# Two PSUM banks as one two-bank tile, or as two one-bank tiles taken in turn, in a fused retention and gated MLP kernel

## The chip, the cores and the metric

The kernel runs on one core of a Trainium2 chip, as one program. The metric is device time in microseconds (us) of one execution. Each engine of the core (TensorE, called PE in the profile; VectorE, DVE; ScalarE, ACT; GpSimd, POOL; SyncE, SP, which issues most transfers) works through its own queue in program order, and waits between engines go over semaphores.

## What is computed

```python
def _attn_ref(q, k, v):                       # 4 batches, 8 heads, 768 tokens, head size 64
    ...
    for t in range(S):
        state = gamma[None, :, None, None] * state + np.einsum('bhd,bhe->bhde', k[:, :, t], v[:, :, t])
        y[:, :, t] = scale * np.einsum('bhd,bhde->bhe', q[:, :, t], state)

def _moe_ref(x, w_val, conv_w, w_out):        # x: the y of all heads side by side, 512 wide
    ...
    for k in range(K):                        # K = 5 taps
        gate_pre += conv_w[k][None, None, :] * xp[:, k:k + S, :]
    gate = 1.0 / (1.0 + np.exp(-gate_pre))
    val = x @ w_val
    return (gate * val @ w_out).astype(np.float32)
```

## The kernel before

The 768 tokens of each batch are cut into 6 chunks of 128, which makes 24 blocks g of one batch and one chunk. The first four blocks (chunk 0) run as `wide_attention`, the others as `attention`: scores (L222) into the PSUM tile `sy`, a mask on DVE (`u`, L232), the state in `z_ps` (L244), a copy of it on ACT (`snap`, L254), and the block's y as the sum of `y_state` and `y_scores` (both L367). DVE multiplies y by a decay and writes it to `x` (`evac`, L435). When a chunk's four blocks are there, the chunk goes through the MLP: `x` is split into a rounded part `xh` (ACT, L444) and a rest `xl` (POOL, L448), DVE sums the taps of the convolution (L550), ACT takes the sigmoid (`gate`, L557).

**Products.** `val` (L565) makes one value tile of 128x512 out of 12 matmuls; DVE multiplies it by the gate (`gated`, L574, the rows `gate<-mm,gate`). The result is split again, into `gvh` (ACT, L581) and `gvl` (POOL, L585), and `outp` (L594) makes one output tile out of 12 matmuls, which ACT copies to `o_sb` (`store`, L604) and SP sends to memory. There are 24 value tiles and 25 output tiles (the last one is made in two halves).

**Banks.** All these sums lie in two PSUM banks, the tile `mm`, 128 x 2 x 512. A helper hands out its halves in turn:

```python
    mm = ps_m.tile([P, 2, 512], F32, name="mm")
    ...
    def bank_of(what):
        banks.append(what)
        return mm[:, (len(banks) - 1) % 2]
```

A value tile and an output tile are mostly summed side by side: PE's queue has matmuls of the one and of the other in alternation. The opening uses the same two banks for `outer`, `turn` and `wide_y`, read by DVE (L302) and ACT (L356, L359). The y of the seven blocks in `PAIRED` (10, 12, ... 22) is summed in both halves of `mm` at once, the y of other blocks in `sy`. The other tiles of PSUM are `sy` (2 banks), `z_ps` (2) and `acc` (2), so that all 8 banks are taken.

**Order.** Every engine's order is fixed by a table of step numbers, `TURNS`, which `plan` turns into the emission order under a manual schedule. Semaphore waits are not written by hand: the layer below places them, from which tiles an instruction reads and writes and which earlier instructions of other engines touched them. Loads of later blocks are held behind products by `hold` (four products back), and all loads and stores go through SP's one queue.

Of the kernel before, what the change touches and what calls it, by code (L numbers as in the profile page):

```python
# [7 lines left out]
F32 = mybir.dt.float32  # L8
# [5 lines left out]
ALU = mybir.AluOpType  # L14
PSUM = bass.MemoryType.PSUM

P = 128
HALF = 64
# [69 lines left out]
def tile_retention_gated_mlp(  # L88
# [32 lines left out]
    nc = tc.nc  # L121
    B, S, DM = out.shape
    NCH = S // P
    HALO = TAPS - 1
# [10 lines left out]
    ps_y = ctx.enter_context(tc.tile_pool(name="ps_y", bufs=1, space=PSUM))  # L135
    ps_s = ctx.enter_context(tc.tile_pool(name="ps_s", bufs=1, space=PSUM))
    ps_a = ctx.enter_context(tc.tile_pool(name="ps_a", bufs=2, space=PSUM))
    ps_m = ctx.enter_context(tc.tile_pool(name="ps_m", bufs=1, space=PSUM))

    tiny = const.tile([P, 1], F32, name="tiny")  # L140
    first_sb = const.tile([P, 512 + NPAIR * TAPS + 36, 2], I32, name="first_sb")
# [12 lines left out]

    z_ps = ps_s.tile([P, 2, B, 2, HALF], F32, name="z_ps")
    sy = ps_y.tile([P, 2, 512], F32, name="sy")
    mm = ps_m.tile([P, 2, 512], F32, name="mm")

    warm = nc.const_aps.tensor(0.0, (P, 1), F32).bitcast(BF16)[:, 0:1]
    steps = []  # L160
# [8 lines left out]
    ys = {}  # L169
    tiles, us, snaps, xs, xh, xl, decs, pos_ps = {}, {}, {}, {}, {}, {}, {0: base}, []  # L170
    rises, falls, begun, falling, turned = {}, {}, [], [], {}

    products = []
    banks, last_of = [], {}

    def bank_of(what):
        banks.append(what)
        return mm[:, (len(banks) - 1) % 2]

    def hold(dma):  # L180

# [23 lines left out]
    def halves(g, what):  # L205

        return tiles[g][:, what].rearrange("p x j (s t) -> p x j s t", s=2)
# [49 lines left out]
    def place(head):  # L257
        return next(
            (x, r, j) for x in range(2) for r in range(2) for j in range(2) if BY_DIM[x][r][j] == head
        )  # L260
# [28 lines left out]
        )  # L289

    def outer(r):
        ps = rises[r] = bank_of(r)
        for i in range(4):
            cols = slice((4 * r + i) * P, (4 * r + i + 1) * P)
            nc.tensor.matmul(
                ps[:, i * P:(i + 1) * P], lhsT=falling[0][:, 0, cols], rhs=falling[0][:, 1, cols],
                start=True, stop=True, skip_group_check=True,
            )
# [19 lines left out]
    def by_token(g, what):  # L318
        return tiles[g][:, what].rearrange("p x j (s e) -> p (x j s) e", s=2)

    def wide_y(g):
        if g not in ys:
            ys[g] = bank_of(g).rearrange("p (a t) -> p a t", t=P)
        v = by_token(g, 2)
        u = us.pop((g, 0)), us.pop((g, 1))
        for ct in range(NPAIR):
            for i, cols in enumerate((LO, HI)):
                x, r, j = place(2 * ct + i)
                nc.tensor.matmul(  # L329
                    ys[g][cols, ct], lhsT=v[:, 2 * ct + i], rhs=u[r][:, 2 * x + j],  # L330
                    start=True, stop=True, skip_group_check=True,
                )
# [13 lines left out]
    turned = {}  # L346

    def turn(g):
        turned[g] = bank_of(g).rearrange("p (a t) -> p a t", t=P)
        kT = tiles[g][:, 1]  # L350
        for x in range(2):
            for j in range(2):
                nc.tensor.transpose(turned[g][:, 2 * x + j], kT[:, x, j], eye_sb)
# [5 lines left out]
        nc.scalar.copy(xs[0][:, :, g, HALO:], ys.pop(g))  # L359

    def area_of(g):
        return ("mm", mm, 0) if g in PAIRED else ("sy", sy, 256)

    def y_mm(g, h, cols, j, s, lhsT, rhs, start):
        _, area, off = area_of(g)
        off += (2 * j + s) * HALF
        return nc.tensor.matmul(  # L367
            area[cols, h, off:off + HALF], lhsT=lhsT, rhs=rhs,
            start=start, stop=True, skip_group_check=True,
        )  # L370

    def behind(area, way):

        was, last = last_of.get(area, (way, None))
        if was != way:
            tc.add_manual_dep(
                nc.tensor.nop().ins, last.ins.name,
                mybir.DependencyInfo(mybir.DependencyClass.Sync, mybir.DependencyReason.DATA),
                reason="row tiles that share a bank",
            )  # L380

    def y_state(g, begins=True):
        if area_of(g)[0] == "mm":
            bank_of(g), bank_of(g)
        q = halves(g, 0)
        behind(area_of(g)[0], 0)
        for s in (1, 0):
            sn = snaps.pop((g, s))
            for j in range(2):
                for h, x, rows, cols in ((0, 0, LO, LO), (1, 0, HI, LO), (1, 1, LO, HI), (0, 1, HI, HI)):  # L390
                    last = y_mm(g, h, cols, j, s, sn[rows, x, j, :], q[rows, x, j, s, :], begins and s == 1 and j == 0)
        last_of[area_of(g)[0]] = 0, last

    def y_scores(g, begins=False):
        v, u = halves(g, 2), us.pop(g)
        behind(area_of(g)[0], 1)
        for s in range(2):
            for j in range(2):
                for h, x, rows, cols in ((0, 0, LO, LO), (1, 0, HI, LO), (1, 1, HI, HI), (0, 1, LO, HI)):
                    last = y_mm(g, h, cols, j, s, v[rows, x, j, s, :], u[rows, x, 2 * j + s, :], begins and s == 0 and j == 0)  # L400
        last_of[area_of(g)[0]] = 1, last

    def first_pos():
        pos_ps.append(ps_a.tile([P, 512], F32, name="acc"))
# [26 lines left out]

    def evac(g):
        b, c = chunks[g]
        _, area, off = area_of(g)
        nc.vector.tensor_tensor(  # L435
            xs[c][:, :, b, HALO:].rearrange("p (h j) t -> p h j t", h=2),
            area[:, :, off:off + 256].rearrange("p h (j t) -> p h j t", t=P),
            decs[c].rearrange("p (h j) t -> p h j t", h=2),
            op=ALU.mult,
        )  # L440

    def round_x(n, ct):
        xh[n, ct] = mlp.tile([P, B, P], F32R, name="xh", bufs=XS)
# [96 lines left out]
    accs, gate, gvs, vps, ops, outs = {}, {}, {}, {}, {}, {}  # L540
# [17 lines left out]

    def val(n, m, i):
        if i == 0:  # L560
            vps[n, m] = bank_of((n, m))
        ct = i % NPAIR
        w, xx = ((wvh, xh), (wvl, xh), (wvh, xl))[i // NPAIR]
        last_of.clear()
        products.append(nc.tensor.matmul(  # L565
            vps[n, m],
            lhsT=w[:, m, ct * P:(ct + 1) * P],
            rhs=xx[n, ct].rearrange("p b t -> p (b t)"),
            start=(i == 0), stop=(i == 3 * NPAIR - 1),
        ))  # L570
# [15 lines left out]

    def outp(n, b, i, cs):
        if i == 0:
            ops[n, b, cs.start] = bank_of((n, b))
        ct = i // 3  # L590
        gvh, gvl = gvs[n, ct]
        gg, w = ((gvh, woh), (gvh, wol), (gvl, woh))[i % 3]
        last_of.clear()
        products.append(nc.tensor.matmul(  # L594
            ops[n, b, cs.start][:, 0:cs.stop - cs.start],
            lhsT=gg[:, b * P:(b + 1) * P],
            rhs=w[:, ct, cs],
            start=(i == 0), stop=(i == 3 * NPAIR - 1),
        ))
# [82 lines left out]
    PAIRED = range(10, NG, 2)  # L682
# [25 lines left out]
    def wide_attention(g):  # L708

        before_block(g)  # L710
        qk, v, k = keys_of(g)
        sc, u, y, bank = Slot("s", 1), [Slot("gvl", GV), Slot("gvl", GV)], Slot("mm", 2), Slot("mm", 2)
        at("PE", 0.5, [qk, "eye"], [bank], turn, g)
        steps[-1].uses.append(held[g])
        at("ACT", 0.5, [bank], [k], take, g)
        steps[-1].uses.append(held[g])
        at("POOL", 1.0, ["small"], [k], decay, g)
        steps[-1].uses.append(held[g])
        at("PE", 1.0, [qk], [sc], wide_scores, g)
        steps[-1].uses.append(held[g])  # L720
        for r in range(2):
            at("DVE", 0.6, [sc, ("fall", r)], [u[r]], wide_mask, g, r)
            steps[-1].uses.append(table_of[r])
        at("PE", 1.0, [v] + u, [y], wide_y, g)
        steps[-1].uses.append(held[g])
        at("PE", 0.6, [v, k] + ["z0"] * (g > 0), [("z", g)] + ["z0"] * (g == 0), wide_state, g)
        steps[-1].uses.append(held[g])
        if g == 0:
            xbufs[0] = Slot("x", XB)
            at("POOL", 0.14, [], [xbufs[0]] + [("x", 0, i) for i in range(B)], new_x, 0)  # L730
        at("ACT", 0.5, [y, xbufs[0]], [("x", 0, g)], wide_evac, g)
        dec_of.setdefault(1, Slot("dec", 2))
        at("ACT", 0.3, ["base", "small"], [dec_of[1], ("dec", 1, g)], table, 1, g)
# [5 lines left out]
    def block(g):  # L739

        y_scores(g, True)
        state(g, 1)
        state(g + 1, 0)
        y_state(g, False)
        scores(g + 1)
# [133 lines left out]
    for r in range(2):  # L879
        bank = Slot("mm", 2)  # L880
        at("PE", 0.26, ["falling"], [bank], outer, r)
        steps[-1].uses.append(falling_of)
        at("DVE", 0.6, [bank, "wide"], [table_of[r], ("fall", r)], weigh, r)
# [124 lines left out]
```

## Time and profile before

| | us |
|---|---|
| median of 3 runs | 251.64 |
| lowest and highest run | 248.99, 251.9 |
| the profiled execution, its own time | 249.62 |
| its span, from the first instruction to the last | 247.9 |
| PE busy | 208.6 |
| DVE busy | 124.1 |
| ACT busy | 116.5 |
| POOL busy | 106.4 |

The durations of the next sections all come from the one profiled execution. Its time is 1.7 us more than its span and 0.8% under the median of the three runs. An engine counts as busy while it executes; waiting in its queue counts as idle, and the profile names the instruction that ended each idle stretch.

### The profile page before, as it was taken

How to read it: one execution, taken by the hardware profiler on the slowest of the kernel's cores; microseconds unless marked ns; L12 is line 12 of the kernel's file. 1: busy time of each engine (PE TensorE's matmuls, PEld its weight loads, DVE VectorE, ACT ScalarE, POOL GpSimd, SP SyncE). 2: the span in 40 equal slices, each digit the busy share in tenths (PEclk: the TensorE clock that was granted, in tenths of full speed). 3: DMA queues.
4: the chain of work that ended last, by engine and by line, in shares of the span. 5: the costliest groups of instructions: out<-in, count | busy, mean ns of one | idle time of the engine just before them, and what ended most of it. 6: DMA issues, size and time to landing. Idle time of an engine off the chain costs nothing.

```text
span 247.9 us, 7469 instructions
## 1 busy us (share of the span) xinstructions
PE 208.6 (84%) x3315; PEld 161.4 (65%) x3315; DVE 124.1 (50%) x188; ACT 116.5 (47%) x241; POOL 106.4 (43%) x99
## 2 busy tenths in 40 slices
PE   4976899996899889888989977898978778778773
PEld 2765688884577768666677865686856556556553
DVE  0755689996665616561636941555835424511000
ACT  4778979796536254344452336343232433302111
POOL 1358988899550538024291500960222540403000
PEclk9999799999799999999999999999999999999999
DMA  6997875587104733760002598010200201111032
GB/s 221 398 405 282 320 256 178 167 317 305 70 24 177 275 127 95 290 215 0 1 3 79 159 384 311 10 45 4 87 0 0 87 0 42 43 42 42 15 115 85
DMA packets 8402, 35.18 MB, mean 142 GB/s; under 512 B 937, under 2 KB 1193, under 8 KB 5810
## 3 DMA queue, kind: packets, MB, share of 16 engines
q1 hardware_dynamic: 8352, 34.66, 38.3%
q8 instruction: 26, 0.43, 0.7%
q10 hardware_dynamic: 18, 0.04, 0.1%
q14 instruction: 6, 0.05, 0.1%
HBM read 28.41 MB, written 6.29 MB: 140 GB/s over the span
## 4 chain that ended last, share of the span: by engine, by line
PE 74%; ACT 11%; DVE 7%; DMA 4%; issue 3%; ACTq 0%; SPq 0%; DVEq 0%
PE mm L594 28%; PE mm L565 28%; ACT o_sb L604 5%; DVE gate L574 5%; PE sy L367 4%; PE mm L367 4%; DMA out_dram<-o_sb 3%; PE sy L222 2%; PE z_ps L244 2%; PE sy L267 1%; PE mm L329 1%; DMA wst<-in_fall_dram 1%; ACT x L359 1%; DVE x L435 1%; ACT acc L488 1%
## 5 line engine op out<-in xcount | busy, mean ns | idle before, releaser
L550 DVE SCALAR_TENSOR_TENSOR acc<-x,cw_sb,acc 128x512 f32<-128x512 f32 x96 | 69.6, 750 | 7.1 <-ACT acc L548 6.2
L585 POOL TENSOR_TENSOR gvl<-gate,gvh 128x512 fp32r<-128x512 f32 x24 | 30.7, 1285 | 67.4 <-ACT gvh L581 57.9
L574 DVE TENSOR_TENSOR gate<-mm,gate 128x512 f32<-128x512 f32 x24 | 16.5, 690 | 63.4 <-PE mm L594 32.9
L594 PE MATMUL mm<-wol,gvh 128*128 128x512 f32 (+1 forms) x100 | 39.7, 405 | 9.5 <-DVE gate L574 5.4
L594 PE MATMUL mm<-woh,gvh 128*128 128x512 f32 (+1 forms) x100 | 39.5, 403 | 3.5 <-DVE gate L574 3.1
L604 ACT COPY o_sb<-mm 128x512 f32<-128x512 f32 (+1 forms) x25 | 13.9, 569 | 60.6 <-PE mm L565 27.5
L448 POOL TENSOR_TENSOR xl<-x,xh 128x512 fp32r<-128x512 f32 x24 | 30.5, 1287 | 26.6 <-ACT xh L444 26.5
L594 PE MATMUL mm<-woh,gvl 128*128 128x512 f32 (+1 forms) x100 | 39.1, 395 | 1.7 <-DVE gate L574 1.7
L565 PE MATMUL mm<-xh,wvh 128*128 128x512 f32 x96 | 31.2, 422 | 4.8 <-ACT o_sb L604 2.7
L212 POOL TENSOR_TENSOR att<-att,first_sb 128x512 f32<-128x512 f32 x24 | 24.9, 1043 | 20.8 <-ACT att L356 8.1
L565 PE MATMUL mm<-xl,wvh 128*128 128x512 f32 x96 | 30.7, 399 | 2.2 <-ACT o_sb L604 1.3
L565 PE MATMUL mm<-xh,wvl 128*128 128x512 f32 x96 | 31.1, 398 | 1.4 <-ACT o_sb L604 1.4
L594 PEld LDWEIGHTS mm<-wol,gvh 128*128 128x128 f32 x100 | 19.0, 190 | 17.1 <-DVE gate L574 7.4
L565 PEld LDWEIGHTS mm<-xh,wvh 128*128 128x128 f32 x96 | 18.0, 194 | 11.1 <-ACT o_sb L604 4.4
L594 PEld LDWEIGHTS mm<-woh,gvh 128*128 128x128 f32 x100 | 19.0, 192 | 9.0 <-DVE gate L574 4.5
L581 ACT CAST gvh<-gate 128x512 fp32r<-128x512 f32 x24 | 14.9, 621 | 20.4 <-DVE gate L574 12.0
L594 PEld LDWEIGHTS mm<-woh,gvl 128*128 128x128 f32 x100 | 19.0, 190 | 6.4 <-DVE gate L574 2.6
L565 PEld LDWEIGHTS mm<-xl,wvh 128*128 128x128 f32 x96 | 17.9, 188 | 7.7 <-ACT o_sb L604 2.2
L557 ACT ACTIVATE gate<-acc 128x512 f32<-128x512 f32 x24 | 14.3, 599 | 17.3 <-DVE acc L550 15.2
L565 PEld LDWEIGHTS mm<-xh,wvl 128*128 128x128 f32 x96 | 17.9, 188 | 6.1 <-ACT o_sb L604 2.2
L254 ACT COPY snap<-z_ps 128x256 f32<-128x256 f32 x40 | 14.1, 373 | 12.3 <-PE z_ps L244 10.9
L548 ACT ACTIVATE acc<-x,cw_sb 128x512 f32<-128x512 f32 x24 | 16.6, 696 | 5.1 <-DVE x L435 3.1
(64 smaller groups left out, 257.5 us busy)
## 6 DMA issues: line engine op xcount, KB each, us to landing
att<-in_att_dram SPq DMA_DIRECT2D x20, 1024.0 KB, 5.5
out_dram<-o_sb SPq DMA_DIRECT2D x23, 256.0 KB, 4.3
wst<-in_w_dram SPq DMA_DIRECT2D x7, 512.0 KB, 6.4
att<-in_att_dram SPq DMA_DIRECT2D x3, 768.0 KB, 8.3
first_sb<-in_first_dram SPq DMA_DIRECT2D x1, 568.0 KB, 6.3
att<-in_att_dram SPq DMA_DIRECT2D x1, 512.0 KB, 4.7
att<-in_att_dram SPq DMA_DIRECT2D x1, 256.0 KB, 7.4
out_dram<-o_sb SPq DMA_DIRECT2D x2, 128.0 KB, 1.7
```

What stands on the lines that cost most here:

```text
L212: nc.gpsimd.tensor_tensor(v, v, vd_sb[:, c, :].unsqueeze(2).broadcast_to([P, 8, HALF]), op=ALU.mult)
L367: return nc.tensor.matmul(area[cols, h, off:off + HALF], lhsT=lhsT, rhs=rhs, start=start, stop=True, skip_group_check=True,)
L448: nc.gpsimd.tensor_tensor(xl[n, ct], xs[n][:, ct, :, HALO:], xh[n, ct].bitcast(F32), op=ALU.subtract)
L548: nc.scalar.mul(acc, x[:, :, 0:P], cw_sb[:, m, 0:1])
L550: nc.vector.scalar_tensor_tensor(acc, x[:, :, k:k + P], cw_sb[:, m, k:k + 1], acc, op0=ALU.mult, op1=ALU.add,)
L557: nc.scalar.activation(gate[n, m], accs.pop((n, m)), AF.Sigmoid)
L565: products.append(nc.tensor.matmul(vps[n, m], lhsT=w[:, m, ct * P:(ct + 1) * P], rhs=xx[n, ct].rearrange("p b t -> p (b t)"), start=(i == ...
L574: nc.vector.tensor_tensor(gv, vps.pop((n, m)), gv, op=ALU.mult)
L581: nc.scalar.copy(gvs[n, m][0], gate[n, m])
L585: nc.gpsimd.tensor_tensor(gvl, gate.pop((n, m)), gvh.bitcast(F32), op=ALU.subtract)
L594: products.append(nc.tensor.matmul(ops[n, b, cs.start][:, 0:cs.stop - cs.start], lhsT=gg[:, b * P:(b + 1) * P], rhs=w[:, ct, cs], start=(i ...
L604: nc.scalar.copy(o_sb[:, 0:step], ops.pop((n, b, cs.start))[:, 0:step])
```

## The change

The pool of the value tiles gets two buffers of one bank each in place of one tile of two banks, and each use asks the pool for a new tile. Steps, their order on every engine and the table `TURNS` stay. A y of a `PAIRED` block takes two such tiles, and since one instruction no longer covers both, `evac` multiplies it in two instructions of 128x256 (L436 in the changed kernel) in place of one of 128x512.

```diff
-    ps_m = ctx.enter_context(tc.tile_pool(name="ps_m", bufs=1, space=PSUM))
+    ps_m = ctx.enter_context(tc.tile_pool(name="ps_m", bufs=2, space=PSUM))
...
-    mm = ps_m.tile([P, 2, 512], F32, name="mm")
...
-    def bank_of(what):
-        banks.append(what)
-        return mm[:, (len(banks) - 1) % 2]
+    def mm_bank():
+        return ps_m.tile([P, 512], F32, name="mm")
...
     def val(n, m, i):
         if i == 0:
-            vps[n, m] = bank_of((n, m))
+            vps[n, m] = mm_bank()
...
     def outp(n, b, i, cs):
         if i == 0:
-            ops[n, b, cs.start] = bank_of((n, b))
+            ops[n, b, cs.start] = mm_bank()
...
     def y_mm(g, h, cols, j, s, lhsT, rhs, start):
-        _, area, off = area_of(g)
-        off += (2 * j + s) * HALF
+        if g not in ysums:
+            ysums[g] = [mm_bank(), mm_bank()] if g in PAIRED else [sy[:, i, 256:512] for i in range(2)]
+        off = (2 * j + s) * HALF
...
+        if g in PAIRED:
+            for h in range(2):
+                nc.vector.tensor_tensor(
+                    x[:, h], y[h][:, 0:256].rearrange("p (j t) -> p j t", t=P), dec[:, h], op=ALU.mult
+                )
```

`outer`, `turn` and `wide_y` take their bank from `mm_bank` in the same way. No instruction changes its place on any engine; what changes is which semaphores some of them wait for. Two places show it. The first is PE's queue late in the program, in the stretch that the profile has at 218.8 to 223 us, where the last matmul of a value tile (`xl,wvh`) is followed by five of an output tile (`woh` and `wol`) and the first ones of the next value tile (`xh,wvh`). DVE_49 and Activation_49 are the semaphores of DVE and ACT. Before:

```order
L565 MATMUL mm<-xl,wvh 128x512
L594 MATMUL mm<-wol,gvh 128x512 [waits DVE_49]
L594 MATMUL mm<-woh,gvl 128x512
L594 MATMUL mm<-woh,gvh 128x512
L594 MATMUL mm<-wol,gvh 128x512
L594 MATMUL mm<-woh,gvl 128x512
L565 MATMUL mm<-xh,wvh 128x512 x2
L565 MATMUL mm<-xh,wvh 128x512 [waits Activation_49]
```

The same stretch of the changed kernel, where val stands in L567 and outp in L596:

```order
L567 MATMUL mm<-xl,wvh 128x512
L596 MATMUL mm<-wol,gvh 128x512
L596 MATMUL mm<-woh,gvl 128x512
L596 MATMUL mm<-woh,gvh 128x512
L596 MATMUL mm<-wol,gvh 128x512
L596 MATMUL mm<-woh,gvl 128x512
L567 MATMUL mm<-xh,wvh 128x512 [waits DVE_49]
L567 MATMUL mm<-xh,wvh 128x512 x3
L596 MATMUL mm<-woh,gvh 128x512 [waits Activation_49]
```

The wait for DVE has moved from the first matmul behind the value tile to the first of the next value tile, five matmuls on, and the wait for ACT from the middle of that value tile to the first matmul of the next output tile.

The second place is DVE's queue at the stretch that the profile has at 82 to 85 us: a gate multiplication, a mask, a tap and the y of a `PAIRED` block. Before:

```order
L574 TENSOR_TENSOR gate<-mm,gate 128x512 [waits Activation_49,Pool_49]
L232 TENSOR_TENSOR u<-sy,tri_sb 128x512 [waits PE_49]
L550 SCALAR_TENSOR_TENSOR acc<-x,cw_sb,acc 128x512
L435 TENSOR_TENSOR x<-mm,dec 128x4x128 [waits PE_49]
L550 SCALAR_TENSOR_TENSOR acc<-x,cw_sb,acc 128x512 [waits DVE_49]
```

And in the changed kernel:

```order
L576 TENSOR_TENSOR gate<-mm,gate 128x512 [waits PE_49,Activation_49]
L230 TENSOR_TENSOR u<-sy,tri_sb 128x512 [waits PE_49]
L552 SCALAR_TENSOR_TENSOR acc<-x,cw_sb,acc 128x512 [waits Activation_49]
L436 TENSOR_TENSOR x<-mm,dec 128x2x128 [waits PE_49]
L436 TENSOR_TENSOR x<-mm,dec 128x2x128
L552 SCALAR_TENSOR_TENSOR acc<-x,cw_sb,acc 128x512 [waits DVE_49]
```

The gate multiplication now names PE's semaphore, and the y is read in two halves.

## Rows read from the trace of the kernel before

**Rows 1.** The page: its first line, and busy time by engine.

```profile
span 247.9 us, 7469 instructions
...
PE 208.6 (84%) x3315; PEld 161.4 (65%) x3315; DVE 124.1 (50%) x188; ACT 116.5 (47%) x241; POOL 106.4 (43%) x99
```

**Rows 2.** Waits by pairs, PE's own: us in total, times, longest.

```profile
PE mm L594 <- DVE gate L574: 10.2, 11, 2.0
PE mm L565 <- ACT o_sb L604: 5.4, 8, 0.7
PE mm L594 <- ACT o_sb L604: 4.2, 5, 1.4
...
PE mm L565 <- DVE gate L574: 2.3, 2, 1.5
PE mm L367 <- ACT o_sb L604: 1.9, 3, 0.8
...
PE mm L367 <- ACT snap L254: 1.1, 1, 1.1
PE mm L367 <- DVE gate L574: 1.0, 2, 0.6
```

**Rows 3.** Timeline, 218.7 to 222.6: start, us, instruction, idle time before it.

```profile
218.77 0.40 PE L565 MATMUL mm<-xl,wvh 128*128 128x512 f32 x1
219.27 0.69 DVE L574 TENSOR_TENSOR gate<-mm,gate 128x512 f32<-128x512 f32 x1 [4.26 <-PE mm L565]
...
220.02 0.50 PE L594 MATMUL mm<-wol,gvh 128*128 128x512 f32 x1 [0.85 <-DVE gate L574]
...
221.05 0.39 PE L594 MATMUL mm<-woh,gvl 128*128 128x512 f32 x1
...
221.28 0.63 PE L565 MATMUL mm<-xh,wvh 128*128 128x512 f32 x2
221.94 0.58 ACT L604 COPY o_sb<-mm 128x512 f32<-128x512 f32 x1 [5.59 <-PE mm L565]
...
222.58 0.73 PE L565 MATMUL mm<-xh,wvh 128*128 128x512 f32 x2 [0.68 <-ACT o_sb L604]
```

**Rows 4.** Timeline, 81.4 to 83 us.

```profile
81.45 0.58 ACT L604 COPY o_sb<-mm 128x512 f32<-128x512 f32 x1
...
82.13 0.69 DVE L574 TENSOR_TENSOR gate<-mm,gate 128x512 f32<-128x512 f32 x1 [3.06 <-ACT o_sb L604]
...
82.88 0.69 PE L367 MATMUL mm<-att,snap 64*64 64x64 f32 x32 [0.61 <-DVE gate L574]
```

**Rows 5.** Busy time by windows: window, its length, each engine, granted clock, DMA.

```profile
26.80:60.00 33.20, 32.50 (x843) 25.99 (x843) 28.65 (x45) 28.22 (x61) 30.44 (x26) 0.95 0.68 247
60.00:72.00 12.00, 9.69 (x124) 6.79 (x124) 9.12 (x15) 5.31 (x11) 6.98 (x7) 0.86 0.26 104
...
200.00:228.00 28.00, 22.56 (x91) 16.17 (x90) 8.33 (x12) 7.06 (x13) 5.12 (x5) 1.00 0.10 37
```

**Rows 6.** Timeline, 64.7 to 68 us, PE.

```profile
64.75 0.63 PE L594 MATMUL mm<-woh,gvl 128*128 128x512 f32 x1
...
65.18 0.63 PE L594 MATMUL mm<-woh,gvh 128*128 128x512 f32 x1
...
67.87 0.34 PEld L244 LDWEIGHTS z_ps<-att 64*64 64x64 f32 x16 [0.65 <-POOL att L212]
```

**Rows 7.** The chain in order of time, at 139.9 us: start, us, what.

```profile
139.87 6.28 DMA out_dram<-o_sb
```

**Rows 8.** Groups by line and form: count, busy, mean ns, idle before, releasers.

```profile
L574 DVE TENSOR_TENSOR gate<-mm,gate 128x512 f32<-128x512 f32 x24 | 16.5, 690 | 63.4 <-PE mm L594 32.9 <-PE mm L565 19.7 <-ACT o_sb L604 10.8
...
L435 DVE TENSOR_TENSOR x<-mm,dec 128x512 f32<-128x512 f32 x7 | 4.8, 690 | 6.7 <-PE mm L367 5.6 <-ACT acc L548 1.0
...
L505 DVE SCALAR_TENSOR_TENSOR top<-first_sb,acc 128x20 int32<-128x20 int32 x1 | 0.2, 176 | 0.1
```

**Rows 9.** Timeline of ACT in the opening, at 17.4 us.

```profile
17.37 0.58 ACT L359 COPY x<-mm 128x512 f32<-128x512 f32 x1 [1.55 <-PE mm L353]
```

More of the change, by code (lines that the diff above doesn't have):

```diff
@@ L173, in tile_retention_gated_mlp @@
     products = []
-    banks, last_of = [], {}
-    def bank_of(what):
-        banks.append(what)
-        return mm[:, (len(banks) - 1) % 2]
+    ysums, last_of = {}, {}
+    def mm_bank():
+        return ps_m.tile([P, 512], F32, name="mm")
     def hold(dma):
@@ L291, in outer @@
     def outer(r):
-        ps = rises[r] = bank_of(r)
+        ps = rises[r] = mm_bank()
         for i in range(4):
@@ L322, in wide_y @@
         if g not in ys:
-            ys[g] = bank_of(g).rearrange("p (a t) -> p a t", t=P)
+            ys[g] = mm_bank().rearrange("p (a t) -> p a t", t=P)
         v = by_token(g, 2)
@@ L348, in turn @@
     def turn(g):
-        turned[g] = bank_of(g).rearrange("p (a t) -> p a t", t=P)
+        turned[g] = mm_bank().rearrange("p (a t) -> p a t", t=P)
         kT = tiles[g][:, 1]
@@ L361, in area_of @@
     def area_of(g):
-        return ("mm", mm, 0) if g in PAIRED else ("sy", sy, 256)
+        return "mm" if g in PAIRED else "sy"
     def y_mm(g, h, cols, j, s, lhsT, rhs, start):
-        _, area, off = area_of(g)
-        off += (2 * j + s) * HALF
+        if g not in ysums:
+            ysums[g] = [mm_bank(), mm_bank()] if g in PAIRED else [sy[:, i, 256:512] for i in range(2)]
+        off = (2 * j + s) * HALF
         return nc.tensor.matmul(
-            area[cols, h, off:off + HALF], lhsT=lhsT, rhs=rhs,
+            ysums[g][h][cols, off:off + HALF], lhsT=lhsT, rhs=rhs,
             start=start, stop=True, skip_group_check=True,
@@ L382, in y_state @@
     def y_state(g, begins=True):
-        if area_of(g)[0] == "mm":
-            bank_of(g), bank_of(g)
         q = halves(g, 0)
-        behind(area_of(g)[0], 0)
+        behind(area_of(g), 0)
         for s in (1, 0):
@@ L391, in y_state @@
                     last = y_mm(g, h, cols, j, s, sn[rows, x, j, :], q[rows, x, j, s, :], begins and s == 1 and j == 0)
-        last_of[area_of(g)[0]] = 0, last
+        last_of[area_of(g)] = 0, last
     def y_scores(g, begins=False):
         v, u = halves(g, 2), us.pop(g)
-        behind(area_of(g)[0], 1)
+        behind(area_of(g), 1)
         for s in range(2):
@@ L400, in y_scores @@
                     last = y_mm(g, h, cols, j, s, v[rows, x, j, s, :], u[rows, x, 2 * j + s, :], begins and s == 0 and j == 0)
-        last_of[area_of(g)[0]] = 1, last
+        last_of[area_of(g)] = 1, last
     def first_pos():
@@ L433, in evac @@
         b, c = chunks[g]
[L434 to L440, printed above, removed]
+        x = xs[c][:, :, b, HALO:].rearrange("p (h j) t -> p h j t", h=2)
+        dec = decs[c].rearrange("p (h j) t -> p h j t", h=2)
+        y = ysums.pop(g)
+        if g in PAIRED:
[3 more added lines that the diff above has]
+                )
+        else:
+            nc.vector.tensor_tensor(
+                x, sy[:, :, 256:512].rearrange("p h (j t) -> p h j t", t=P), dec, op=ALU.mult
+            )
     def round_x(n, ct):
```

## The prediction, made before the changed kernel ran

> **What bounds the kernel now.** I read the page first: PE is busy for 208.6 us of a span of 247.9, and DVE, ACT and POOL for half of it or less [rows 1]. So PE sets the end, and its 39 idle us are what can be won. Then the waits by pairs, for PE alone: the reader should see that most of this idle time ends with an instruction that reads the tile `mm`, a gate multiplication on DVE or a copy to `o_sb` on ACT. Six pairs of a product or a y against such a reader add up to 10.2 + 5.4 + 4.2 + 2.3 + 1.9 + 1.0 = 25.0 us in 31 stops [rows 2].
>
> Third, the timeline around one stop of each kind, since a read of PSUM need not stop PE at all [rows 3]. The last matmul of a value tile (L565) is issued at 218.77, DVE reads the tile from 219.27 to 219.96, and PE starts again at 220.02. But what it starts with is L594 `wol,gvh`, a matmul in the middle of the output tile that was being summed beside the value tile, in the other bank. It doesn't need what DVE reads. The reverse wait is there too: the output tile has its last matmul at 221.05, which ends at 221.44, and ACT's copy begins at 221.94, right behind two matmuls (L565) that belong to the next value tile. It waited for writes to a bank that it doesn't read. And two readers wait for each other: at 82.13 the gate multiplication begins when ACT's copy of the other bank is done [rows 4]. So in this kernel every instruction on `mm` waits as if the two banks were one thing. The two-bank tile is taken as one; the rows agree with that everywhere I looked.
>
> **What the change removes.** Each buffer of the pool is a tile of its own, and the order of the changed kernel shows the waits where the banks ask for them: five matmuls behind the value tile in place of the next one, and four behind the output tile. What a stop costs is more than its idle time, because matmuls overlap. In an undisturbed run the second of two matmuls is issued 0.63 - 0.40 = 0.23 us after the first [rows 3]. At the gate's stop the distance is 220.02 - 218.77 = 1.25, which costs 1.02 for an idle time of 0.85. At the copy's stop it is 222.58 - 221.51 = 1.07, which costs 0.84 for 0.68. So a stop costs about 0.165 us beyond its idle time. I add to the 31 stops one of 1.1 us that the profile puts down to a copy of the state on ACT [rows 2], because that copy stands in ACT's queue behind an `o_sb` copy that had to wait. The sum of what goes is 25.0 + 1.1 + 32 x 0.165 = **31.4 us**.
>
> **Is the true wait hidden?** At the first place, PE needs 1.25 us from the issue of the value tile's last matmul to its restart behind the read. In the new order the next value tile's first matmul comes six steps after that matmul, 6 x 0.233 = 1.40 us; it isn't stopped, with 0.15 to spare. Behind the output tile the need is 0.39 + 0.58 and twice some 0.05 for the handover, 1.07, and the cover is five steps, 1.17. These are small margins, and they hold only where the reader's engine is free when the tile is done.
>
> **What stays.** Five terms, each with its bounds.
> - Between 60 and 72 us PE idles for 2.3 us [rows 5], two of the stops above. But at 67.87 PE is just waiting for POOL's decay of a loaded block [rows 6], and POOL comes earlier only as far as its own inputs do. I let 1.2 us stay; the bounds are 0 and 2.7, the stops with their restarts.
> - The longest stop on ACT's copy, 1.4 us, is behind a store that takes 6.28 us from its issue at 139.87 [rows 7], since the copy needs that buffer of `o_sb`. The stop moves to the next value tile's start. I leave 1.1; bounds 0.4 and 1.5.
> - Of the 1.1 us at the state copy, 0.5 stays, since that copy has work of its own to do; bounds 0 and 1.1.
> - A y of a `PAIRED` block starts soon behind the tiles whose banks it takes [rows 4], with less cover than products have: 0.3 in all, 0 to 1.
> - New lateness. DVE idles for 63.4 us before its 24 gates, 2.6 us each [rows 8]; PE gains 31.4 us over the some 188 us in which products run, 1.3 us for the 7.8 us between two gates. On average half of DVE's slack is left, but some gates and copies will find their engine in the middle of a tap or a cast, and loads land later as seen from PE. If a quarter of the 49 reads comes late by half an instruction of 0.7 us, that is 4.3 us. I take 2.0; bounds 0 and 6.
>
> What stays is 1.2 + 1.1 + 0.5 + 0.3 + 2.0 = 5.1 us.
>
> **What is added.** Seven instructions on DVE. One of 512 columns takes 690 ns and one of 20 takes 176 [rows 8], so 1.045 ns per column and 423 ns for 256 columns: the two halves take 846, and the seven y together 7 x 0.156 = 1.1 us more. I cost it at nothing: DVE's idle time before its gates hides it, and the first half frees its bank 0.27 us earlier than the whole did. Without that cover it would be the 1.1 us, which the bound of 6 above includes. Transfers, SBUF and the number of PSUM banks don't change.
>
> **The opening.** ACT waits 1.55 us at 17.37 for a transpose in the other bank (L353), though the y that it copies was ready before [rows 9]. It is busy from there on, so its chain can move up by as much; but from 26.8 to 60 us PE is busy for 32.5 of 33.2 us, and DVE, ACT and POOL for 28 to 30 [rows 5]. What comes early must pass all four. I take 0.5 us, between 0 and 1.2.
>
> The sum: 31.4 - 5.1 + 0.5 = 26.8 us off the execution's own time of 249.62, that is **222.8 us**. I count against the profiled execution, where the durations are from; the median of the three runs is 2.0 us higher, so the top of the range gets 2.0 more. At best the stays are 0.4 and the opening gives 1.2, and half clock in 60 to 72 us (granted 0.86 there [rows 5]) doesn't come, some 1.5 us: 34 us off, 215.6. At worst 12.3 us stay and the opening gives nothing: 19.1 off, 230.5, and with the 2.0, 232.5.
>
> **Rivals.**
> - *Other queues become the bound.* The margins of 0.10 and 0.15 us are lost at most reads, because DVE or ACT is busy when a tile is done. If the 49 reads are late by 0.3 us on average, 14.7 us come back: 222.8 + 14.7 - 2.0 = 235.5. For it: the small margins, and the dense stretch before 60 us. Against it: of 63.4 us of idle time before gates, 32.9 + 19.7 end with PE [rows 8]; and late in the program, from 200 to 228 us, DVE and ACT are busy for 8.3 and 7.1 of 28 us [rows 5].
> - *No change.* The stops only move from the running product to the next tile in the same bank, or the layer below still ties the two buffers together. Then 249.6, and the y in halves makes it 249.6 to 250.7. For it: PE works in order, so that any wait stops all products behind it. Against it: the order of the changed kernel, which has five and four matmuls before those waits. The Trainium skill, in "TensorE: Matmul & The Clock Gate", section "HAM oscillation — how this bites in real kernels", reports a matmul kernel in which double-buffering PSUM gave nothing more (126.6 to 125.5 us); by that ratio this one would go to 247.5. The rows speak against carrying that over: here PE has 25 us of stops that end with reads of PSUM [rows 2].
> - *Slower: the clock.* PE is granted full clock from 200 to 228 us, with all its stops, and 0.86 on average in 60 to 72 [rows 5], where matmuls are issued 65.18 - 64.75 = 0.43 us apart [rows 6], half speed (1.2 of 2.4 GHz), in place of 0.23. If denser products that change banks more often lost the clock, each of the 588 product matmuls at half clock would cost 0.20 us; from 26.8 / 0.20 = 134 of them on the kernel would be slower than before, and with a third of them it would take 222.8 + 196 x 0.20 = 262 us. Against it: the window with the half clock is one in which PE idles for 2.3 of 12 us, and the change removes idle time. The skill's same page, section "A second HAM failure mode: psum-queue depth-cycling", says that cycling through PSUM banks can leave PE idling often enough to lose its clock again and again. This trace doesn't show it: granted clock 1.00 in a stretch with a stop every few us [rows 5].
>
> **Chances.** The forecast 0.85, other queues 0.08, no change 0.04, the clock 0.03. About 2% is what a measurement of this kernel can tell from no change, since its runs lie 248.99 to 251.9 us. So faster by over 2% has 0.93, within 2% 0.04, slower 0.03. For 8 in 10, the range takes the bounds worked out above, 215 to 232.
>
> **What would show it.** In the changed kernel's profile: PE's busy time near 203 us (32 restarts shorter) in a span near 221; the pairs of L596 and L567 against gate and `o_sb` down from 25 us to under 6; no gate that waits for an `o_sb` copy; a product's last matmul followed within 0.3 us by the next one of the other product. The y in halves should take some 0.42 us each. If stops of 0.1 to 0.5 us stand at the first matmuls of tiles, with DVE or ACT busy just before the read, the term of new lateness was too small. If stores or loads end them, that is what I have missed. If stops of 0.85 and 0.68 us are still in the middle of products, the waits are not what I take them for.

## The result, and the profile after

The changed kernel takes 214.94 us (median of 4 runs, 214.05 to 215.32) beside 250.31 us for the kernel before on the same chip (median of 4): a ratio of 0.861, 95% interval 0.852 to 0.869. In a later run it was 213.40 against 249.81, 0.854 (0.849 to 0.858). So the change takes 35 to 36 us off, where 26.8 were forecast; the time lies 0.06 us under the low end of the range. The profiled execution took 214.05 us.

The page of the changed kernel, its first line and the busy times:

```profile
span 212.3 us, 7475 instructions
...
PE 200.1 (94%) x3315; PEld 162.3 (76%) x3315; DVE 124.8 (59%) x195; ACT 116.4 (55%) x241; POOL 106.4 (50%) x99
```

Against [rows 1], PE's idle time went from 39.3 us (247.9 - 208.6) to 12.2, and its busy time fell by 8.5 although it executes the same 3315 matmuls. Both halves need an explanation. The waits by pairs of PE (us in total, times, longest) show the first:

```profile
PE acc L406 <- DMA wst<-in_fall_dram: 3.3, 1, 3.3
PE z_ps L242 <- POOL att L210: 1.5, 1, 1.5
PE mm L327 <- DVE gvl L309: 1.1, 1, 1.1
PE mm L567 <- ACT o_sb L606: 0.9, 1, 0.9
PE sy L366 <- issue: 0.6, 1, 0.6
...
PE mm L366 <- DVE gate L576: 0.5, 1, 0.5
PE mm L366 <- ACT snap L252: 0.3, 1, 0.3
```

The 32 counted stops, 26.1 us with the one put down to the state copy [rows 2], have become three of 1.7 us together. What leads the list now is the opening. One stop is new: 0.58 us at 115.91, in the middle of a block's y, for which the profile shows no cause (`issue`). The timeline of one value tile (start, us, instruction, idle time before it) answers to [rows 3]:

```profile
190.76 0.39 PE L567 MATMUL mm<-xl,wvh 128*128 128x512 f32 x1
...
190.99 0.39 PE L596 MATMUL mm<-wol,gvh 128*128 128x512 f32 x1
...
191.26 0.69 DVE L576 TENSOR_TENSOR gate<-mm,gate 128x512 f32<-128x512 f32 x1 [2.64 <-PE mm L567]
...
191.91 0.40 PE L596 MATMUL mm<-woh,gvl 128*128 128x512 f32 x1
192.00 0.80 PEld L567 LDWEIGHTS mm<-xh,wvh 128*128 128x128 f32 x4
192.15 1.09 PE L567 MATMUL mm<-xh,wvh 128*128 128x512 f32 x4
192.35 0.59 ACT L606 COPY o_sb<-mm 128x512 f32<-128x512 f32 x1 [2.55 <-PE mm L596]
```

PE goes on 0.23 us after the value tile's last matmul, with the output tile, while DVE reads. DVE's read ends at 191.95, the weights of the next value tile are loaded from 192.00, and its first matmul comes at 192.15, on PE's beat of 0.23 us. That is 0.20 us behind the end of the read; in [rows 3] PE restarted 0.06 behind it. So some 0.15 us are to spare, as the prediction had it: that is how narrow the true wait is, and it held. ACT's copy now waits for its own tile (PE L596) and no longer for the other one. The groups by line and form (count, busy, mean ns, idle before with releasers) answer to [rows 8]:

```profile
L576 DVE TENSOR_TENSOR gate<-mm,gate 128x512 f32<-128x512 f32 x24 | 16.5, 689 | 41.0 <-PE mm L567 31.3 <-ACT acc L550 7.2 <-PE mm L596 1.8
...
L436 DVE TENSOR_TENSOR x<-mm,dec 128x256 f32<-128x256 f32 x14 | 5.3, 418 | 3.9 <-PE mm L366 3.9
```

Gates wait for matmuls of value tiles (L567, 31.3 us), which they read, no `o_sb` copy is among the releasers, and the time before a gate went from 63.4 to 41.0 us. Three windows (length, each engine's busy time, granted clock, DMA) answer to [rows 5]:

```profile
26.00:58.00 32.00, 31.90 (x880) 25.94 (x871) 30.48 (x48) 28.32 (x63) 31.02 (x27) 1.00 0.72 267
58.00:70.00 12.00, 12.00 (x287) 9.55 (x286) 10.11 (x17) 7.06 (x15) 8.91 (x8) 1.00 0.37 129
160.00:190.00 30.00, 30.00 (x159) 23.92 (x158) 17.54 (x26) 13.79 (x24) 11.42 (x9) 1.00 0.12 44
```

PE is never idle in the second and third, and the clock is 1.00 throughout, where before it was 0.95 and 0.86 in the first two.

### The profile page after: what moved, and what is told of

Read it like the earlier page. It is cut to its first block, busy times and chain, and to the rows that moved or that the text cites. A ratio compares the mean times of both kernels' runs of the same rounds, so it can differ in the third digit from the quotient of the medians.

```text
span 212.3 us, 7475 instructions
## 1 busy us (share of the span) xinstructions
PE 200.1 (94%) x3315; PEld 162.3 (76%) x3315; DVE 124.8 (59%) x195; ACT 116.4 (55%) x241; POOL 106.4 (50%) x99
## 4 chain that ended last, share of the span: by engine, by line
PE 86%; ACT 4%; DMA 4%; issue 1%; DVE 1%; POOL 1%; SPq 0%; POOLq 0%; ACTq 0%
PE mm L567 32%; PE mm L596 31%; PE sy L366 6%; PE sy L220 5%; PE z_ps L242 4%; PE mm L366 4%; DMA out_dram<-o_sb 3%; PE sy L265 2%; DMA wst<-in_fall_dram 1%; PE mm L327 1%; ACT o_sb L606 1%; PE z_ps L283 1%; DVE gvl L309 1%; POOL rest L519 1%; ACT acc L486 1%
## 5 line engine op out<-in xcount | busy, mean ns | idle before, releaser
L576 DVE TENSOR_TENSOR gate<-mm,gate 128x512 f32<-128x512 f32 x24 | 16.5, 689 | 41.0 <-PE mm L567 31.3
L596 PE MATMUL mm<-woh,gvh 128*128 128x512 f32 (+1 forms) x100 | 38.5, 393 | 0.0
L596 PE MATMUL mm<-woh,gvl 128*128 128x512 f32 (+1 forms) x100 | 38.4, 388 | 0.0
L596 PE MATMUL mm<-wol,gvh 128*128 128x512 f32 (+1 forms) x100 | 38.1, 390 | 0.0
L606 ACT COPY o_sb<-mm 128x512 f32<-128x512 f32 (+1 forms) x25 | 14.1, 569 | 35.7 <-PE mm L596 31.9
L567 PE MATMUL mm<-xh,wvl 128*128 128x512 f32 x96 | 30.6, 395 | 0.0
L567 PE MATMUL mm<-xl,wvh 128*128 128x512 f32 x96 | 30.3, 397 | 0.0
L567 PE MATMUL mm<-xh,wvh 128*128 128x512 f32 x96 | 29.1, 403 | 0.9 <-ACT o_sb L606 0.9
L596 PEld LDWEIGHTS mm<-woh,gvh 128*128 128x128 f32 x100 | 18.7, 188 | 5.0 <-ACT o_sb L606 0.7
L583 ACT CAST gvh<-gate 128x512 fp32r<-128x512 f32 x24 | 14.9, 622 | 13.4 <-DVE gate L576 7.0
L596 PEld LDWEIGHTS mm<-woh,gvl 128*128 128x128 f32 x100 | 18.8, 188 | 4.1
L567 PEld LDWEIGHTS mm<-xh,wvh 128*128 128x128 f32 x96 | 17.6, 188 | 5.3 <-ACT o_sb L606 1.2
L596 PEld LDWEIGHTS mm<-wol,gvh 128*128 128x128 f32 x100 | 18.7, 188 | 3.9
L567 PEld LDWEIGHTS mm<-xl,wvh 128*128 128x128 f32 x96 | 17.9, 188 | 4.5 <-POOL xl L450 0.4
L567 PEld LDWEIGHTS mm<-xh,wvl 128*128 128x128 f32 x96 | 18.0, 188 | 4.0
L252 ACT COPY snap<-z_ps 128x256 f32<-128x256 f32 x40 | 14.1, 374 | 10.1 <-PE z_ps L242 8.6
```

Source lines behind the costliest of these rows:

```text
L567: products.append(nc.tensor.matmul(vps[n, m], lhsT=w[:, m, ct * P:(ct + 1) * P], rhs=xx[n, ct].rearrange("p b t -> p (b t)"), start=(i == ...
L576: nc.vector.tensor_tensor(gv, vps.pop((n, m)), gv, op=ALU.mult)
L583: nc.scalar.copy(gvs[n, m][0], gate[n, m])
L596: products.append(nc.tensor.matmul(ops[n, b, cs.start][:, 0:cs.stop - cs.start], lhsT=gg[:, b * P:(b + 1) * P], rhs=w[:, ct, cs], start=(i ...
L606: nc.scalar.copy(o_sb[:, 0:step], ops.pop((n, b, cs.start))[:, 0:step])
```

## The experiments

Three theories stood before the runs. **T1**: three kinds of wait across the banks, which the one tile caused, make up the whole gain, each with its share: PE behind reads of the other bank, reads behind matmuls into the other bank, and reads behind reads. **T2**: only the first kind counts. **T3**: something else in the change (two buffers, halves, the place of the banks, the clock) carries the gain. The first four runs keep the changed kernel's buffers and halves, and put waits back by dependencies. They ran beside the kernel before and not beside the changed kernel, whose two medians are 1.5 us apart; a difference to the changed kernel is known no better than that. Cut to its core, the code is:

```python
def link(one, other):                       # instruction `one` waits for `other`
    tc.add_manual_dep(one.ins, other.ins.name, ...)
def wrote(one):                             # around every matmul into a tile mm
    if "PE after reads" in LINKS:           # e2, e5
        for other in fresh.values(): link(one, other)
        fresh.clear()
    wrote_last[:] = [one]
    return one
def read(one, engine):                      # around every read of a tile mm
    if "reads after PE" in LINKS:           # e3, e5
        link(one, wrote_last[0])
    if "reads after reads" in LINKS:        # e4, e5
        for e, other in latest.items():
            if e != engine: link(one, other)
    fresh[engine] = latest[engine] = one
    return one
```

**PE waits for reads of either bank.** 

> Two buffers and halves as in the changed kernel, but each matmul into a value or output tile also waits for the latest reads of the other bank, as before. T1 (three false waits together made the stops, each with its share): the stops of PE come back, but shorter than before, since the reads themselves no longer wait for the other bank's matmuls or for each other: a gate's stop of 1.02 us stays 1.02, an output copy's stop of 0.84 goes to about 0.4. 13 gate stops x 1.0 + 16 copy stops x 0.4 = 19 us above the changed kernel's 214.9: about 234, 228 to 240. T2 (only PE's waits behind reads count): all of it comes back, about 250, 246 to 252. T3 (the gain is not these waits but the tiles' new place or the clock): 213 to 217.

Measured: 228.31 us (227.49 to 229.33), ratio to before 0.914 (0.909 to 0.918), 13.4 above the changed kernel's 214.94. T2 and T3 both fall. T1's direction holds, at the edge of its range; with free reads the stops are fewer (7 and 3 behind gates and copies in output tiles, 11 and 5 before):

```profile
PE mm L626 <- DVE gate L606: 4.9, 7, 1.1
...
PE mm L626 <- ACT o_sb L636: 2.6, 3, 1.4
PE mm L597 <- ACT o_sb L636: 1.8, 4, 0.7
```

**Reads wait for PE's matmuls into either bank.** 

> The changed kernel, but each read of a value or output tile also waits for the last matmul that was put in PE's queue on either bank. T1: a copy comes up to 0.47 us later, so that its end passes the first matmul of the next tile in that bank by 0.3 to 0.4 us where the margin was 0.10 to 0.15; gates follow their tile's last matmul directly and don't change. 16 to 24 copies x 0.3 = 5 to 7 us above 214.9: about 221, 217 to 228. T2 (only PE's waits behind reads count): 214 to 217. T3 (not these waits): 213 to 217.

Measured: 229.03 us (228.04 to 229.99), ratio 0.916 (0.912 to 0.921), 14.1 above. T2 falls again, and T1's size was wrong by a factor of two. The timeline at a copy:

```profile
180.81 0.39 PE L626 MATMUL mm<-woh,gvl 128*128 128x512 f32 x1
...
182.91 0.40 PE L597 MATMUL mm<-xl,wvh 128*128 128x512 f32 x1
183.10 0.58 ACT L636 COPY o_sb<-mm 128x512 f32<-128x512 f32 x1 [3.88 <-PE mm L597]
...
183.74 0.50 PE L626 MATMUL mm<-woh,gvh 128*128 128x512 f32 x1 [0.44 <-ACT o_sb L636]
```

The copy's own tile has its last matmul at 180.81, which ends at 181.20. The copy waits on for matmuls of the value tile (L597), starts 1.9 us behind the end of its tile and ends at 183.68; PE stops for 0.44 us, some 0.7 with its restart (below) and not the 0.3 of the expectation. In the changed kernel the same copy starts 0.04 us behind its tile. The expectation put the delay at 0.47 us at most and gave gates none. By the timelines of the two kernels, 18 of the 49 reads come 0.59 to 1.87 us later behind their own tile than in the changed kernel, gates as well as copies, and the pairs have four stops of products behind gates, 2.4 us in all. In the changed kernel 31 of the 49 reads start within 0.12 us of the end of their tile, here 8. The distance from a tile's end to its read adds up to 34 us in the changed kernel, to 60 us here and to 64 us in the kernel before. So reads held up by 0.5 us each on average, some by nearly 2, bring back 14 us. This run does not test the small margin of 0.10 to 0.15 us by itself, since most of its delays are far larger.

**DVE and ACT wait for each other's reads.** 

> The changed kernel, but the gate on DVE and the copy on ACT each also wait for the other engine's latest read of a bank. T1: DVE idles 2.6 us before a gate on average, so most of these waits are over when the gate comes; 1 to 2 us above 214.9: 215 to 217.5. T2 and T3: 214 to 216, which this run alone does not tell from T1.

Measured: 216.32 us (215.88 to 217.23), ratio 0.866 (0.862 to 0.870): 1.4 above 214.94, in T1's range, and 2.9 above the 213.40 of the later run. The third kind is the smallest; the interval of the ratio overlaps that of the changed kernel's first run (0.852 to 0.869) and not that of its later one (0.849 to 0.858), so that its size stays open.

**All three kinds at once.** 

> The changed kernel with all three kinds of waits across the banks put back at once; buffers, halves and orders stay as changed. T1 and T2 (the waits are the whole gain): before's time comes back, 250, 247 to 253, with stops of 0.85 and 0.68 us in the middle of products and the stretches of half clock near 27 to 30 and 64 to 68 us. T3 (something else in the change carries part of the gain: two buffers, halves, the bank's place): clearly under 245; at 213 to 217 the waits would carry nothing.

Measured: 251.82 us (250.01 to 252.41), ratio 1.007 (1.003 to 1.011). T3 falls: the waits are the whole gain. In the profiled execution (250.01 us, the fastest of its seven) PE's waits are those of [rows 2] again, pair by pair:

```profile
PE mm L626 <- DVE gate L606: 10.3, 11, 2.0
PE mm L597 <- ACT o_sb L636: 5.4, 8, 0.7
PE mm L626 <- ACT o_sb L636: 4.1, 5, 1.3
...
PE mm L597 <- DVE gate L606: 2.3, 2, 1.5
PE mm L395 <- ACT o_sb L636: 1.9, 3, 0.8
```

The three kinds alone cost 13.4 + 14.1 + 1.4 = 28.9 us, together 251.82 - 214.94 = 36.9. Against the 213.40 of the later run of the changed kernel it is 33.4 and 38.4. So 5 to 8 us come only when more than one kind is there; no run had just two of them. Part of it is the clock: its mean over a run was 0.986 to 0.993 here, 0.999 to 1.000 with the first or the third kind alone and 0.992 to 1.000 with the second. In the profiled execution half clock came back only at the second place; its windows at 26.8 to 60, 60 to 72 and 64 to 66 us:

```profile
26.80:60.00 33.20, 31.65 (x844) 25.31 (x844) 29.52 (x46) 28.09 (x62) 31.10 (x27) 1.00 0.73 254
60.00:72.00 12.00, 10.05 (x152) 7.27 (x152) 9.11 (x15) 5.74 (x12) 6.87 (x6) 0.86 0.20 83
64.00:66.00 2.00, 2.00 (x5) 1.61 (x6) 2.00 (x4) 1.43 (x3) 1.27 (x2) 0.50 0.00 0
```

The expectation had it at 27 to 30 us as well. And 0.7% over the kernel before is more than the interval allows for nothing; the next run shows that it is not the halves. A few waits more than before remain in this kernel (four of the 24 gates name ACT in addition), which could be it; that stays open.

**The halves alone**, in the kernel before:

```diff
-        nc.vector.tensor_tensor(
...
+        if g in PAIRED:
+            for h in range(2):
+                nc.vector.tensor_tensor(x[:, h], y[:, h], dec[:, h], op=ALU.mult)
+        else:
+            nc.vector.tensor_tensor(x, y, dec, op=ALU.mult)
```

> The kernel before, with one two-bank tile, but the y of the seven paired blocks multiplied in two halves of 128x256 as in the changed kernel. T1 (the waits between the banks are the whole gain): same time as before, 250.0, 249 to 251; a half takes 0.42 us in place of 0.69 for the whole, 7 x 0.15 = 1.1 us more on VectorE, hidden in its idle time; were it on the path, 251.1. T3 (the halves carry a part of the gain, since their first half frees a bank earlier): under 248.5.

Measured: 250.17 us beside 250.85 for before, ratio 1.0006 (0.9974 to 1.0039). The halves cost and give nothing that could be told from noise, 0.4% or 1 us either way.

**PE's idle time before the half clock**, in the kernel before:

```diff
-        products.append(nc.tensor.matmul(
...
+        times = 6 if not begun_outs else 1
+        begun_outs.append(i)
+        for again in range(times):
+            product = nc.tensor.matmul(
...
+                start=(i == 0), stop=(i == 3 * NPAIR - 1 or again < times - 1),
...
+        products.append(product)
```

> The kernel before, but the first matmul of the first output tile is issued six times in place of once (each starts the sum anew, so the result is the same). The five more take 5 x 0.23 = 1.2 us of the 1.95 us in which PE stands idle up to 62.8 us, so that nothing else should move. Theory A (the half clock at 64.5 to 68 us comes from PE's idling before it, and goes with it): granted clock 1.00 from 64 to 68, 1.6 us less than before: 248.4, 247.5 to 249.2. Theory B (that stretch has another cause, or the stop of 0.85 us before it is enough): granted clock still near 0.5 there, 250.0, 249.4 to 250.8.

Measured: 248.00 us beside 250.85, ratio 0.991 (0.987 to 0.995), 2.2 us less by the ratio. Its timeline, and its windows 60 to 72 and 64 to 68 us:

```profile
59.86 1.66 PE L597 MATMUL mm<-woh,gvh 128*128 128x512 f32 x6 [0.85 <-DVE gate L574]
62.37 0.50 PE L597 MATMUL mm<-wol,gvh 128*128 128x512 f32 x1 [0.85 <-DVE gate L574]
...
64.71 0.40 PE L597 MATMUL mm<-wol,gvh 128*128 128x512 f32 x1
64.94 0.40 PE L597 MATMUL mm<-woh,gvh 128*128 128x512 f32 x1
```

```profile
60.00:72.00 12.00, 10.61 (x205) 7.84 (x205) 9.57 (x15) 6.89 (x14) 7.97 (x7) 1.00 0.24 85
64.00:68.00 4.00, 4.00 (x76) 3.16 (x77) 3.70 (x6) 2.24 (x5) 2.65 (x3) 1.00 0.02 6
```

Theory A holds: five useless matmuls in idle time make the kernel faster. Where the kernel before issues matmuls 0.43 us apart [rows 6], this one issues them 0.23 apart, at a granted clock of 1.00. So the half clock after 64 us was the stops' own consequence, and the change removes it with them. The profiled execution of this run also has full clock from 26.8 to 60 us, which before had not, so the 2.2 us need not all be of the one place. But that is not what took away the half clock after 64 us: the run with all three kinds of waits has full clock from 26.8 to 60 us too, and 0.50 from 64 to 66. The granted clock of whole runs agrees: 0.979 to 0.993 in 23 runs of the kernel before, 0.990 to 1.000 in the 12 of this one.

**Six buffers of o_sb** in the changed kernel (`bufs=4` becomes `bufs=6`), since the longest stop left, 0.87 us at 132.88, ends with a copy that waited 1.02 us for a store (`<-DMA out_dram<-o_sb` in the trace). 

> The changed kernel with six buffers of o_sb in place of four. The longest stop left late in the changed kernel, 0.87 us before a value tile at 132.9, goes, if the copy there waits for a buffer whose store has not landed: 0.87 + 0.17 = 1.0 us less, 213.9, 213.2 to 214.6. Rival (the copy or PE has another wait that ends as late): 214.6 to 215.4, the stop still there.

Measured: 212.83 us (211.97 to 214.09), ratio 0.852 (0.847 to 0.856), just below the expected range, and no stop on `o_sb` in its waits. That was 2.1 below the changed kernel's median from the earlier run, so both went once more, side by side:

> The changed kernel once more, beside the next run on the same chip: 214.9, 214 to 216.

> The changed kernel with six buffers of o_sb, beside the changed kernel itself on the same chip. If the stop of 0.87 us is all that goes, 1.0 us less than the run beside it. If the buffers also let later copies start earlier, up to 2.1 us less, which is what the two medians of separate runs differ by (214.94 and 212.83). Rival (the chips differ, the buffers do nothing): within 0.4 us of it.

Measured: 213.40 for the changed kernel (212.73 to 214.80), below the 214 to 216 expected, and 213.39 with six buffers (211.90 to 215.03), so no difference to be told, though the stop (0.79 us in this profile of the changed kernel) is gone. In the two profiles the opening differs by more than that. The end of PE's wait for POOL in the changed kernel, then with six buffers:

```profile
24.03 0.46 PE L242 MATMUL z_ps<-att 64*64 64x64 f32 x16 [1.51 <-POOL att L210]
```

```profile
25.43 0.46 PE L242 MATMUL z_ps<-att 64*64 64x64 f32 x16 [1.51 <-POOL att L210]
```

From there to the end of the span it is 211.0 - 24.0 = 187.0 and 211.2 - 25.4 = 185.8 us, 1.2 less, as one stop with its restart would give. But in the first profile with six buffers the same stretch is 210.6 - 23.8 = 186.8, with another stop of 0.38 us. Whether six buffers are worth 1 us stays undecided; no version here is shown to beat the changed kernel.

## Why the prediction was right in kind and short in size

**What bounds the kernel** was right: PE, stopped by waits for a bank that it doesn't need. With only the waits put back, the pairs of [rows 2] come back to 0.1 us each.

**What is removed** was mis-sized at one step: "a stop costs about 0.165 us beyond its idle time". I took the distance to the matmul that restarts, and not the one behind it. The timeline of the kernel before, one row after the gate's stop in [rows 3]:

```profile
220.36 0.39 PE L594 MATMUL mm<-woh,gvl 128*128 128x512 f32 x1
220.59 0.39 PE L594 MATMUL mm<-woh,gvh 128*128 128x512 f32 x1
```

The restarting matmul of 220.02 takes 0.50 us and the next one comes 0.34 behind it, then 0.23 again. So a stop in a product costs 0.165 + 0.11 = 0.27 us beyond its idle time. The two traces agree: from before to after, the same matmul comes earlier by 27.92 us at 215.42, by 29.03 at 220.02 and by 29.98 at 222.58, 1.11 and 0.95 us for a gate's and a copy's stop that I put at 1.02 and 0.84. With 26 such stops in products [rows 2] that is 2.6 us too few. (It is one reason why PE's busy time fell below the 203 us that I named; the half clock below is another.)

**What stays** was put too high, 5.1 us where some 2.2 are left: the three stops, 1.7 us, and 3 x 0.165. Between 60 and 72 us nothing stays, not 1.2: POOL came as much earlier as PE. The store's stop is 0.87 and not 1.1, the state copy's 0.33 and not 0.5, a `PAIRED` y's 0.45 and not 0.3. The new lateness, 2.0, is nil: beyond these three no gate or copy comes late enough to stop PE, in line with the 41 us that DVE still idles before its gates. That is 2.9 us. The prediction had no term for the stop without a shown cause at 115.91; by the lead of the same matmuls it costs 0.6 us, net.

**The clock** was kept out of the sum, as a bound of 1.5 us for one place. It belonged in it: the stretch of half clock stands right behind the longest stops that the sum removes, and the run with repeated matmuls ties the two. There was a second stretch, in the 0.95 that [rows 5] have from 26.8 to 60 us, which I did not look into. The window 28 to 30 us of before:

```profile
28.00:30.00 2.00, 2.00 (x20) 1.15 (x23) 1.88 (x3) 2.00 (x8) 2.00 (x2) 0.50 1.03 418
```

By the lead of the same matmuls, the changed kernel gains 1.2 us in the first stretch and 1.5 in the second beyond the stops there. The first is not in every profile of the kernels with the stops, and no run was made for it: that it goes with them is argued, and 1.2 of these 2.7 us belong to the one execution that was profiled.

**The other terms** held. The opening gave 0.43 us at the first product (0.5 forecast). Halves take 418 ns each (423) and cost nothing. Three stops on the `PAIRED` y's read, which I had not counted, gave some 0.6 by the lead of the same matmuls. Not forecast either: behind the start of PE's last matmul the kernel before needs 4.0 us to its end and the changed kernel 3.4, 0.6 us less.

With these sizes the sum is 26.8 + 2.6 + 2.9 + 2.7 + 0.6 = 35.6 us, against 249.62 - 214.05 = 35.6; the new stop and the shorter end, 0.6 each, cancel. That it closes so well proves little for the single terms, which were sized afterwards from the same two executions. The prediction's best case is 31.4 - 0.4 + 1.2 + 1.5 = 33.7 us off, which it rounds to 34; the change gave more than that, by the restarts and the first stretch of half clock.

**The rivals** fell. Other queues did not become the bound, though the one run with late reads lost 14 us by them. "No change" fell with a gain that the false waits explain: the measured kernel in the Trainium skill, "TensorE: Matmul & The Clock Gate", section "HAM oscillation — how this bites in real kernels", gained nothing from double-buffered PSUM, and here the rows of stops were the better guide. The clock went the other way from the third rival: taking banks in turn with hardly a stop between had a granted clock of 1.00. The same page of the Trainium skill, section "A second HAM failure mode: psum-queue depth-cycling", puts a lost clock down to small idle times of PE between groups while it cycles through banks. Here the run with repeated matmuls agrees with the part on idle time, and the changed kernel shows cycling through two banks at 1.00.

## What to carry to other kernels

When an engine stops in the middle of work that doesn't need the thing it waits for, look at what the waiting layer takes as one thing: split the tile along the pieces that are really shared, and check the order of waits, since the cover behind the true wait (here five matmuls, with some 0.15 us to spare) decides what is won. Count a stop by its whole cost, up to where the beat is regular again, and the clock that it may lose behind it. Where several false waits sit on the same resource, removing one can leave much of the loss: here either of the two large ones, put back alone, cost 13 to 14 us of the 36.

## What the runs showed that I had not expected

Five repeated matmuls in an idle stretch of the kernel before made it 0.9% faster (0.987 to 0.995), and in its profile PE kept full clock behind them.

The opening, whose instructions are the same in all of them, ends with PE's restart at 25.55, 24.03, 23.80 and 25.43 us in four profiles of the changed kernel and of the one with six buffers. The two profiles of the same changed kernel are 1.5 us apart, more than the stop that I tried to remove. What sets it was not tried.
